# A fused attention and FFN block: moving the last q tile, two layer norms, PSUM banks and a scaling

## The chip, the cores and the metric

One Trainium2 chip, one core. The metric is the device time of one execution in microseconds, the median over the runs. Every matmul runs at the full granted TensorE clock (mean 1.000).

## The reference

One block with adaptive layer norm, linear attention and a SwiGLU FFN, on 2048 rows of 1024:

```python
mod = (silu(c) @ w_mod).reshape(1, 6, 1, -1); sa, ca, ga, sb, cb, gb = ...
h  = layernorm(x) * (1 + ca) + sa
q, k, v = split(h @ wqkv) into 32 heads of 32
phi(t) = where(t > 0, t + 1, exp(t)) + 1e-6
kv = sum_s phi(k) v ;  z = sum_s phi(k)                    # per head
o  = (phi(q) @ kv) / (phi(q) @ z + 1e-6)
x  = x + ga * (o @ wo)
h  = layernorm(x) * (1 + cb) + sb
x  = x + gb * ((silu(h @ w_gate) * (h @ w_up)) @ w_down)   # F = 3584
```

All inputs and the output are bfloat16.

## The kernel before

The program is a list of operations for five in-order queues (TensorE "pe", ScalarE "act", VectorE "dve", GpSimd "pool", and "sp", which issues the DMAs). A helper records every operation and derives the waits from the bytes, and for PSUM from the whole bank, that it touches. So nearly all instructions have the line of that helper, L176, and are told apart by their tiles. The order within a queue is the order in which the code calls the helpers.

**Stages.** The rows are cut into 4 chunks of 512 (each of 4 row tiles `st` of 128).

1. *Start and chunk 0's q (0 to 29 us).* Layer norm of chunk 0, transposes, and `q_phase_chunk0`: seven of the eight q tiles (`nt` 0 to 6) are accumulated in seven PSUM banks `qb = [1, 2, 3, 4, 6, 7, 5]`, one input slice `dt` at a time (`q_part`), while the modulation vectors are still being computed: `mod_sc` are 16 or 32 matmuls with one column into bank 0, `fin_sa` reads them out, `bias_mm` (32 one-column matmuls) and `bias_fin` give a bias for the q tiles. The eighth tile (`nt` 7) follows in bank 0. `h0_shift` then adds the shift to four slices of the transposed input `HT`. `q_phi` evicts a q tile with two ScalarE instructions (Exp into `E1`/`E1X`, Relu into `RL`/`RLX`), `q_min` and `q_add` make phi of them on VectorE (about 0.2 and 0.33 us an instruction) and write `PQT`.
2. *k of chunk 0, then chunks 1 to 3 (29 to 126 us).* Each group is 8 matmuls of 128x512. A chunk is 8 k groups and 8 q groups (chunk 0 has its q groups before). I write c1k2 for the k group 2 of chunk 1. `phi_evac` evicts a group: ScalarE's Exp into one of four slots of `E1` (for q a Relu too); after every second group `phi_flush` does VectorE's part of both: `min`, `min`, then for k one `scalar_tensor_tensor` each into `PKT` (it reads PSUM too, so a k group's bank comes free only there), for q one `tensor_tensor` each. `next_bank` gives the PSUM bank: a ring of eight for the first 40 groups, then a ring of five for chunk 3, because banks 0, 6 and 7 are kept for the next stage.
3. *Side work of stage 2.* The dictionaries `kside` (chunk 0's k), `s1`, `s2`, `s3` (chunks 1 to 3) say behind which group which helpers are called: the layer norm of the chunk after (`ln1_stats_ops`: two `bn_stats` and an aggregate on VectorE; `act_stats`: two passes of 1024 columns on ScalarE, Identity and Square with a sum; `ln1_xn`: the normalisation), its transposes by DMA (`th_dma`, one for each row tile, into `HT`), the scaling and shift of the eight slices of the transposed chunk (`th_mod(ch, dt)`; chunk 1's all on VectorE, of the others the odd ones on ScalarE), and a part of the modulation that VectorE sums up from a 2 MB block of `w_mod` in `STG` (`macc`, eight passes of 1024 columns into `ACC`). `macc_split` writes `MHL` and sends it through a DMA transpose; behind that in the DMA queue stands the load of the next 2 MB into `STG`, which chunk 3's `macc` needs.
4. *G (126 to 186 us).* 16 groups of 16 matmuls, `g_evac`, the reciprocal of the denominator, which goes out to memory and comes back broadcast as `RB` (two loads of four DMAs, 512 KB each), `scale_pq` (PQT times RB, one hg a time), `kvt_mm`, `m_mm`.
5. *Output projection, second layer norm and FFN (186 to 824 us).* 

The rings and the side work that matter here:

```python
return (1, 2, 3, 4, 6, 7, 5, 0)[i % 8] if i < 40 else i % 5 + 1        # next_bank
add(s2, 13, macc_split)
add(s2, 13, lambda: P.dma("stg1", STG[:], wmv[:, :, 4096:5120]))
add(s3, 4 + kt, lambda kt=kt: macc(STG, kt))                            # kt 0 to 7
```

Of the kernel before, what the change touches and what calls it, by code (L numbers as in the profile page):

```python
# [5 lines left out]
FP32 = mybir.dt.float32  # L6
BF16 = mybir.dt.bfloat16
U8 = mybir.dt.uint8
ACT = mybir.ActivationFunctionType
# [253 lines left out]
def bass_adaLN_cond__linear_attn_block__swiglu_ffn__prompt_kernel(  # L263
# [22 lines left out]
    with ExitStack() as es:  # L286
# [59 lines left out]
        RL = T("rl", 188 * KB, [128, 4, 512], BF16)  # L346
        E1X = T("e1x", 192 * KB, [128, 4, 512], BF16)
        RLX = T("rlx", 196 * KB, [128, 4, 512], BF16)
        ACC = T("acc", 192 * KB, [128, D], FP32)
        MHL = T("mhl", 196 * KB, [128, 2, D], BF16)  # L350
        MHLT = T("mhlt", 192 * KB, [128, 2 * NDT, 128], BF16)
# [351 lines left out]
        def next_bank():  # L703
            i = qk_ctr[0]
            qk_ctr[0] += 1
            return (1, 2, 3, 4, 6, 7, 5, 0)[i % 8] if i < 40 else i % 5 + 1

        def q_group(ch, nt):
            buf, bank = ch % 2, next_bank()
# [39 lines left out]
        def mod_row_b(bank, i, dst):  # L749
# [3 lines left out]
            P.wait_for("sp", [wr])  # L753
            P.dma("mdr%d" % i, dst[:], MDR[i].unsqueeze(0).to_broadcast([128, D]))

        def q_slot(nt):
            return (E1, RL) if nt < 4 else (E1X, RLX)

        def q_phi(nt, bank):
            for buf, fn_ in zip(q_slot(nt), (ACT.Exp, ACT.Relu)):  # L760
                P.act("activation", out=buf[:, nt % 4, :], in_=PS[:, bank, :], func=fn_, bias=BIASQ[:, nt:nt + 1])

        def q_min(nts):
            for nt in nts:
                e = q_slot(nt)[0][:, nt % 4, :]
                P.dve("tensor_scalar", out=e, in0=e, scalar1=1.0, scalar2=1e-6, op0=ALU.min, op1=ALU.add)

        def q_add(nts):
            for nt in nts:
                e, r = q_slot(nt)  # L770
                P.dve("tensor_tensor", out=PQT[:, nt, 0:512], in0=r[:, nt % 4, :], in1=e[:, nt % 4, :], op=ALU.add)

        def q_phase_chunk0():
            qb = [1, 2, 3, 4, 6, 7, 5]
            fin_ca(2, 2)
            for dt in (2, 3):
                h0_first(dt, "dve")
            for nts, dts in ((range(3), (0,)), (range(3), (1,)), ((3, 4, 5, 6), (0, 1))):
                for nt in nts:
                    q_part(nt, qb[nt], dts)  # L780
            for nt in range(7):
                if nt == 4:
                    mod_sc(WCA, 8, range(4, 8))
                    fin_ca(4, 4)
                    for dt in (4, 5):
                        h0_scale_only(dt)
                q_part(nt, qb[nt], (2, 3))
            act_stats(4, (0,))
            for nt in range(7):
                if nt == 6:  # L790
                    mod_sc(WSA, 0, range(6, 8))
                    fin_sa(6, 2)
                    for dt in (6, 7):
                        h0_scale(dt)
                q_part(nt, qb[nt], (4, 5))
            mod_sc(WSA, 0, range(4, 6))
            fin_sa(4, 2, True)
            for dt in (4, 5):
                h0_shift(dt)
            for nt in range(7):  # L800
                if nt == 2:
                    bias_mm((4, 5))
                q_part(nt, qb[nt], (6,))
            for nt in range(7):
                if nt == 1:
                    mod_sc(WSA, 0, range(4), range(4))
                if nt == 3:
                    mod_sc(WSA, 0, range(4), range(4, 8))
                    fin_sa(0, 4, True)
                    ln_ops[1][0]()  # L810
                if nt == 5:
                    bias_mm(range(4))
                    bias_fin()
                q_part(nt, qb[nt], (7,))
            ln_ops[1][1]()
            ln_ops[1][2]()
            ln1_rstd1(5)
            for i, dt in enumerate((4, 5, 0, 1, 2, 3, 6, 7)):
                P.pe("matmul", out=PS[:, 0, :], lhsT=WQK[:, dt, 896:1024], rhs=HT[:, 0, dt, :], start=(i == 0),
                     stop=(i == 7))  # L820
            for dt in range(4):
                h0_shift(dt)
            ln1_xn(5)
            th_dma(5)
            for nt in range(2):
                q_phi(nt, qb[nt])
            act_stats(4, (1,))
            for nt in range(2, 8):
                q_phi(nt, qb[nt] if nt < 7 else 0)
            for f in ln_ops[2]:  # L830
                f()
            act_var(4)
            pool_pow(4)
            for f in ln_ops[3]:
                f()
            ln1_rstd2(6)
            ln1_xn_sum(4)
            th_dma(4)
            q_min((0, 1))
            for st in (6, 7):  # L840
                ln1_xn(st)
                th_dma(st)
            q_add((0, 1))
            for nts in ((2, 3), (4, 5)):
                q_min(nts)
                q_add(nts)
            qk_ctr[0] = 0

        def add(d, k, f):
# [2 lines left out]
        kside = {}  # L852
        ln_ops = [ln1_stats_ops(4 + jj) for jj in range(4)]

        for c0 in (0, 256):
            for dt in range(NDT):
                add(kside, 1, lambda dt=dt, c0=c0: th_mod(1, dt, c0, c0 + 256))
        add(kside, 1, lambda: q_min((6, 7)))
        add(kside, 1, lambda: q_add((6, 7)))
        for jj, k in ((0, 3), (1, 4)):  # L860
            add(kside, k, lambda jj=jj: act_stats(10 + jj))
        q_phase_chunk0()
        for st in range(12, 16):
# [44 lines left out]
            add(s1, 2, lambda jj=jj: th_dma(8 + jj))  # L908
        for i, dt in zip([9, 9, 10, 10, 10, 11, 11, 11], range(NDT)):
            add(s1, i, lambda dt=dt: th_mod(2, dt))  # L910
        ln_half(3, s1, 8, 8, 11)
        for jj in range(4):
            add(s1, 13 + jj // 2, lambda jj=jj: ln1_xn(12 + jj))
            add(s2, 0, lambda jj=jj: th_dma(12 + jj))
        for dt in range(NDT):
            add(s2, 6 + dt, lambda dt=dt: th_mod(3, dt))
        for kt in range(NDT):
# [52 lines left out]
        def den():  # L970
            for hg in range(NHG):
                for ch in range(NCH):
                    P.pe("matmul", out=PS[32 * ch:32 * ch + 32, 7, :], lhsT=ZSEL[:, hg * 32:hg * 32 + 32],
                         rhs=PQT[:, hg, ch * 512:(ch + 1) * 512], start=(hg == 0), stop=(hg == NHG - 1),
                         skip_group_check=True)
            P.dve("tensor_scalar", out=DEN[:], in0=PS[:, 7, :], scalar1=1e-6, scalar2=None, op0=ALU.add)
            P.dve("reciprocal", out=RCP[:], in_=DEN[:])
            P.dve("tensor_copy", out=RCB[:], in_=RCP[:])
            wr = [P.dma("rdr%d" % ch, RDR[:, ch * 512:(ch + 1) * 512], RCB[32 * ch:32 * ch + 32, :])
                  for ch in range(NCH)]  # L980
            P.wait_for("sp", wr)
            for gh in range(2):
                outs = [RB[32 * hh:32 * hh + 32, 4 * gh:4 * gh + 4, :] for hh in range(4)]
                ins = [RDR.rearrange("(g x) s -> x g s", x=4)[hh, 4 * gh:4 * gh + 4].unsqueeze(0).to_broadcast([32, 4, S])
                       for hh in range(4)]

                def fn(e, outs=outs, ins=ins):
                    return [e.dma_start(out=o_, in_=i_) for o_, i_ in zip(outs, ins)]

                P.add("sp", fn, reads=[], writes=outs, lane="rb%d" % gh, ninc=4, tag="rb")  # L990

        def scale_pq(hg):
            P.dve("tensor_tensor", out=PQT[:, hg, :], in0=PQT[:, hg, :], in1=RB[:, hg, :], op=ALU.mult)
# [1 line left out]
        def kvt_mm(half):  # L995
            for h in range(4):
                for dt in range(NDT):
                    for g in range(4):
                        c0 = 512 * half + 128 * g + 32 * h
                        P.pe("matmul", out=PS[32 * g:32 * g + 32, 6, 32 * h:32 * h + 32], lhsT=WV[:, dt, c0:c0 + 32],  # L1000
                             rhs=G[:, dt, c0:c0 + 32], start=(h == 0 and dt == 0), stop=(dt == NDT - 1),
                             skip_group_check=True)
            P.dve("tensor_copy", out=KVT[:, half, :], in_=PS[:, 6, 0:128])

        def m_mm(half, nh, banks):
            for k in range(4):
# [31 lines left out]
        for g in range(16):  # L1038
            g_group(g)
            while ev < g + 1 - (3 if g < 4 else 2 if g < 6 else 1):  # L1040
                g_evac(ev)
                ev += 1
            if g == 0:
                z_row()
                for f in range(2):
                    wo_load(f)
            if g == 1:
                mod_red()
                mod_fin_col(2, True)
                den()  # L1050
            if 6 <= g <= 9:
                fold_ga(2 * (g - 6))
                fold_ga(2 * (g - 6) + 1)
            if g == 10:
                kvt_mm(0)
            if 11 <= g < 13:
                m_mm(0, g - 11, [MB, 7, G_BANKS[4], 6])
            if 7 <= g < 15:
                scale_pq(g - 7)
            if g == 10:  # L1060
                P.dma("stgx1", STGX[0][:], wmv[:, :, 3072:4096])
        g_evac(15)
# [185 lines left out]
```

## Time and profile before

| | |
|---|---|
| median of 3 runs | 827.69 us (827.62 to 828.37) |
| the profiled execution: its time, its span | 827.71 us, 826.0 us |
| TensorE busy, granted clock | 816.3 us, 1.000 |
| VectorE, ScalarE, GpSimd busy | 312.2, 197.0, 41.0 us |
| DMA | 119.32 MB |
| chain that ended last | 98% matmuls |

The span runs from the first to the last instruction; 1.7 us of the execution lie around it. Busy time is the union of an engine's instructions. Matmuls are pipelined: one of 128x512 shows as 0.38 us, but the next starts 0.216 us after it. A trace lacks a few per cent of the matmul records, so a missing start is not a pause.

### The profile page before, as it was taken

To read this page: it belongs to the slowest core of one execution; us is meant where nothing else is said; L and a number is where in the kernel's file an instruction comes from. 1 tells how busy PE (TensorE), PEld (TensorE's weight loads), DVE (VectorE), ACT (ScalarE), POOL (GpSimd) and SP (SyncE) were. 2 spreads that over 40 slices of the span, in tenths; PEclk is the share of its full clock that TensorE was granted. 3 is DMA by queue.
4 is the path that set the end of the run, shared out by engine and by line. 5 is a ranking of instruction groups with operands and counts; after the bars stand their busy time and mean duration, and the time that the engine had idled before them with its cause. 6 is when DMAs were issued, how large, how long until landed. Compare 5 with 4: busy or idle time off the path is not lost.

```text
span 826.0 us, 10436 instructions
## 1 busy us (share of the span) xinstructions
PE 816.3 (99%) x4243; PEld 375.9 (46%) x4322; DVE 312.2 (38%) x672; ACT 197.0 (24%) x338; POOL 41.0 (5%) x58
## 2 busy tenths in 40 slices
PE   8999999999999999999999999999999999999998
PEld 4544444444444444444444444444444444444444
DVE  5798988477945521111221112122111111221111
ACT  4758642123341111011111101111110111111011
POOL 1110000000130000020000003000000300000000
DMA  9969756865698995600455570045557004553000
GB/s 316 297 139 223 167 159 149 181 175 211 149 253 245 296 249 153 166 26 26 136 151 151 153 174 25 23 131 153 151 152 182 27 19 126 151 152 88 0 26 26
DMA packets 199392, 119.32 MB, mean 144 GB/s; under 512 B 58024, under 2 KB 183088, under 8 KB 199344
## 3 DMA queue, kind: packets, MB, share of 16 engines
q1 hardware_dynamic: 199328, 118.65, 53.8%
q8 instruction: 34, 0.56, 0.3%
q14 instruction: 14, 0.11, 0.0%
q10 hardware_dynamic: 16, 0.00, 0.0%
HBM read 100.67 MB, written 4.33 MB: 127 GB/s over the span
## 4 chain that ended last, share of the span: by engine, by line
PE 98%; issue 1%; DMA 0%; DVE 0%; POOL 0%; SPq 0%
PE ps L176 98%; DMA xres<-in_A_x_dram 0%; POOL rstd L176 0%; DVE xres L176 0%; DVE stats L176 0%; SPq L176 0%; DVE ht L176 0%; DVE ve L176 0%; DVE mv L176 0%; DVE modcol L176 0%
## 5 line engine op out<-in xcount | busy, mean ns | idle before, releaser
L176 PE MATMUL ps<-h2t,gug 128*128 128x512 bf16 x878 | 210.1, 379 | 0.9
L176 PE MATMUL ps<-h2t,guu 128*128 128x512 bf16 x878 | 209.9, 379 | 0.9
L176 DVE TENSOR_TENSOR at<-sg,ps 128x512 bf16<-128x512 bf16 x112 | 77.0, 687 | 282.8 <-PE ps L176 270.6
L176 ACT ACTIVATE sg<-ps 128x512 bf16<-128x512 f32 x112 | 66.9, 597 | 309.7 <-PE ps L176 298.3
L176 PEld LDWEIGHTS ps<-h2t,guu 128*128 128x128 bf16 x896 | 87.7, 98 | 105.7
L176 PEld LDWEIGHTS ps<-h2t,gug 128*128 128x128 bf16 x896 | 87.6, 98 | 105.5
L176 PE MATMUL ps<-wd_a,at 128*128 128x512 bf16 (+1 forms) x502 | 111.9, 377 | 0.5
L176 PE MATMUL ps<-ht,wqk 128*128 128x512 bf16 x499 | 110.7, 379 | 0.9 <-DVE ht L176 0.2
L176 PE MATMUL ps<-wd_b,at 128*128 128x512 bf16 (+1 forms) x377 | 84.6, 377 | 0.4
L176 PEld LDWEIGHTS ps<-wd_a,at 128*128 128x128 bf16 x512 | 50.1, 98 | 59.6
L176 DVE TENSOR_TENSOR ut<-att,gb_b 128x512 bf16<-128x512 bf16 (+1 forms) x32 | 13.6, 426 | 167.5 <-ACT att L176 167.5
L176 PEld LDWEIGHTS ps<-ht,wqk 128*128 128x128 bf16 x512 | 49.2, 98 | 58.9 <-DVE ht L176 1.0
L176 ACT ACTIVATE att<-ps 128x512 bf16<-128x512 f32 (+1 forms) x32 | 17.4, 591 | 182.1 <-PE ps L176 182.1
L176 PEld LDWEIGHTS ps<-wd_b,at 128*128 128x128 bf16 x384 | 37.6, 98 | 44.7
L176 PE MATMUL ps<-pk,xres 128*128 128x512 bf16 x250 | 55.4, 379 | 0.6 <-issue 0.5
L176 PE MATMUL ps<-mw,pqt 128*128 128x512 bf16 x249 | 55.4, 379 | 0.5 <-issue 0.2
L176 POOL TENSOR_SCALAR h2t<-h2t,modcol 128x512 bf16<-128x512 bf16 x32 | 26.5, 846 | 383.0 <-DMA h2t<-xn 383.0
L176 ACT ACTIVATE e<-ps 128x512 bf16<-128x512 f32 x56 | 33.3, 611 | 31.8 <-PE ps L176 15.8
L176 ACT ACTIVATE junk<-xres 128x1024 bf16<-128x1024 bf16 x26 | 27.6, 1063 | 45.9 <-DVE xres L176 34.2
L176 PEld LDWEIGHTS ps<-mw,pqt 128*128 128x128 bf16 x256 | 24.8, 98 | 30.0 <-issue 0.5
L176 PEld LDWEIGHTS ps<-pk,xres 128*128 128x128 bf16 x256 | 24.6, 98 | 30.1 <-issue 1.3
L176 DVE SCALAR_TENSOR_TENSOR xres<-ps,xres 128x512 bf16<-128x512 f32 x32 | 21.5, 688 | 11.6 <-PE ps L176 11.3
(111 smaller groups left out, 337.8 us busy)
## 6 DMA issues: line engine op xcount, KB each, us to landing
gug<-in_B_w_gate_dram SPq DMA_DIRECT2D x56, 512.0 KB, 4.0
guu<-in_B_w_up_dram SPq DMA_DIRECT2D x56, 512.0 KB, 5.3
xres<-in_A_x_dram SPq DMA_DIRECT2D x20, 256.0 KB, 4.4
rb<-recip_den SPq DMA_DIRECT2D x8, 512.0 KB, 11.7
stgx<-in_w_mod_dram SPq DMA_DIRECT2D x2, 2048.0 KB, 9.3
wd_a<-in_B_w_down_dram SPq DMA_DIRECT2D x4, 1024.0 KB, 7.7
out_dram<-xres SPq DMA_DIRECT2D x31, 128.0 KB, 1.7
xres<-in_A_x_dram SPq DMA_DIRECT2D x3, 1024.0 KB, 6.5
```

What stands on the lines that cost most here:

```text
L176: return getattr(e, method)(**kw)
```

## The change

Five things are moved; the arithmetic stays.

- *Chunk 0's q.* Tile 0 of q is finished first, ScalarE copies it as fp32 to a new tile `QRAW`, and the eighth tile is accumulated in the bank that this frees. Its eight matmuls stand between the pieces of the last shift products (`mod_sc`, `bias_mm`), where the last round of `q_part` stood. Both passes of `act_stats(4)`, its variance, `pool_pow(4)` and the normalisation of row tile 4 come earlier, before the q evictions. The evictions run in the order `QORD`.
- *Banks.* `next_bank` has other rings for the first 40 groups.
- *Chunk 1's scaling.* Still called behind c0k1, but with 8 half-width instructions for the slices 0 to 3 and 4 full-width ones for 4 to 7, in place of 16 halves; the last two pairs of chunk 0's q go behind c0k3 (before, only the last pair came this late, right behind the scaling); `act_stats(10)` and `(11)` one group later.
- *Chunk 3's layer norm.* From behind groups 8, 9 and 11 of chunk 1 to behind 12, 13 and 14; the normalisation from 13 and 14 to 15 and the first group of chunk 2; the transposes from behind c2k0 to behind c2k1.
- *RB.* Loads of 3, 3 and 2 hg; the third is issued by SP behind a wait for the eviction of `kvt_mm(0)`; `scale_pq(6)` and `(7)` at G groups 14 and 15 in place of 13 and 14.

```diff
         def next_bank():
...
-            return (1, 2, 3, 4, 6, 7, 5, 0)[i % 8] if i < 40 else i % 5 + 1
+            if i < 24:
+                return (0, 2, 3, 4, 6, 7, 5, 1)[i % 8]
+            if i < 40:
+                return (0, 2, 3, 4, 6, 1, 7, 5, 0, 2, 3, 1, 4, 6, 7, 5)[i - 24]
+            return i % 5 + 1
...
-            act_stats(4, (0,))
...
             for nt in range(7):
-                if nt == 1:
+                q_part(nt, qb[nt], (7,))
+                if nt == 0:
+                    P.act("activation", out=QRAW[:], in_=PS[:, qb[0], :], func=ACT.Copy)
+                    act_stats(4)
+            for i, dt in enumerate(range(NDT)):
+                if i == 1:
                     mod_sc(WSA, 0, range(4), range(4))
-                if nt == 3:
+                if i == 3:
                     mod_sc(WSA, 0, range(4), range(4, 8))
+                    ln_ops[1][0]()
                     fin_sa(0, 4, True)
-                    ln_ops[1][0]()
-                if nt == 5:
+                    ln_ops[1][1]()
+                    act_var(4)
+                    pool_pow(4)
+                if i == 5:
                     bias_mm(range(4))
                     bias_fin()
-                q_part(nt, qb[nt], (7,))
-            ln_ops[1][1]()
+                P.pe("matmul", out=PS[:, qb[0], :], lhsT=WQK[:, dt, 896:1024], rhs=HT[:, 0, dt, :], start=(i == 0),
+                     stop=(i == 7))
...
+            ln1_xn_sum(4)
+            th_dma(4)
             ln1_xn(5)
             th_dma(5)
...
-            q_add((0, 1))
-            for nts in ((2, 3), (4, 5)):
-                q_min(nts)
-                q_add(nts)
+            q_add(QORD[0:2])
+            q_pair(2)
...
-        for c0 in (0, 256):
-            for dt in range(NDT):
-                add(kside, 1, lambda dt=dt, c0=c0: th_mod(1, dt, c0, c0 + 256))
-        add(kside, 1, lambda: q_min((6, 7)))
-        add(kside, 1, lambda: q_add((6, 7)))
-        for jj, k in ((0, 3), (1, 4)):
+        for dt, c0, c1 in ([(dt, 0, 256) for dt in range(4)] + [(dt, 256, 512) for dt in range(4)]
+                           + [(dt, 0, 512) for dt in range(4, 8)]):
+            add(kside, 1, lambda dt=dt, c0=c0, c1=c1: th_mod(1, dt, c0, c1))
+        for i in (4, 6):
+            add(kside, 3, lambda i=i: q_pair(i))
+        for jj, k in ((0, 4), (1, 5)):
             add(kside, k, lambda jj=jj: act_stats(10 + jj))
...
-        ln_half(3, s1, 8, 8, 11)
+        ln_half(3, s1, 12, 12, 14)
         for jj in range(4):
-            add(s1, 13 + jj // 2, lambda jj=jj: ln1_xn(12 + jj))
-            add(s2, 0, lambda jj=jj: th_dma(12 + jj))
+            add(s1 if jj < 2 else s2, 15 if jj < 2 else 0, lambda jj=jj: ln1_xn(12 + jj))
+            add(s2, 1, lambda jj=jj: th_dma(12 + jj))
...
+            rb_load(0, 3)
+            rb_load(3, 6)
...
             if g == 10:
-                kvt_mm(0)
+                P.wait_for("sp", [kvt_mm(0)])
+                rb_load(6, 8)
...
-            if 7 <= g < 15:
+            if 7 <= g < 13:
                 scale_pq(g - 7)
+            elif g == 14:
+                scale_pq(6)
+            elif g == 15:
+                scale_pq(7)
```

Here `q_pair(i)` is `q_min` and `q_add` of the tiles `QORD[i:i + 2]`, and `ln_half(ch, d, k_act, k_dve, k_fin)` puts `act_stats`, `bn_stats` and the final sums of a chunk behind the groups `k_act`, `k_dve` and `k_fin`.

More of the change, by code (lines that the diff above doesn't have):

```diff
@@ L348, in bass_adaLN_cond__linear_attn_block__swiglu_ffn__prompt_kernel @@
         RLX = T("rlx", 196 * KB, [128, 4, 512], BF16)
+        QRAW = T("qraw", 202 * KB, [128, 512], FP32)
         ACC = T("acc", 192 * KB, [128, D], FP32)
@@ L754, in mod_row_b, with q_phi @@
             P.dma("mdr%d" % i, dst[:], MDR[i].unsqueeze(0).to_broadcast([128, D]))
+        QORD = (1, 2, 3, 4, 5, 6, 7, 0)
         def q_slot(nt):
-            return (E1, RL) if nt < 4 else (E1X, RLX)
-        def q_phi(nt, bank):
+            i = QORD.index(nt)
+            bufs = (E1, RL) if i < 4 else (E1X, RLX)
+            return [t[:, i % 4, :] for t in bufs]
+        def q_phi(nt, src):
             for buf, fn_ in zip(q_slot(nt), (ACT.Exp, ACT.Relu)):
-                P.act("activation", out=buf[:, nt % 4, :], in_=PS[:, bank, :], func=fn_, bias=BIASQ[:, nt:nt + 1])
+                P.act("activation", out=buf, in_=src, func=fn_, bias=BIASQ[:, nt:nt + 1])
         def q_min(nts):
             for nt in nts:
-                e = q_slot(nt)[0][:, nt % 4, :]
+                e = q_slot(nt)[0]
                 P.dve("tensor_scalar", out=e, in0=e, scalar1=1.0, scalar2=1e-6, op0=ALU.min, op1=ALU.add)
@@ L770, in q_add, with q_pair @@
                 e, r = q_slot(nt)
-                P.dve("tensor_tensor", out=PQT[:, nt, 0:512], in0=r[:, nt % 4, :], in1=e[:, nt % 4, :], op=ALU.add)
+                P.dve("tensor_tensor", out=PQT[:, nt, 0:512], in0=r, in1=e, op=ALU.add)
+        def q_pair(i):
+            q_min(QORD[i:i + 2])
+            q_add(QORD[i:i + 2])
         def q_phase_chunk0():
@@ L804, in q_phase_chunk0 @@
             for nt in range(7):
-                if nt == 1:
+                q_part(nt, qb[nt], (7,))
[4 more added lines that the diff above has]
+                if i == 1:
                     mod_sc(WSA, 0, range(4), range(4))
-                if nt == 3:
+                if i == 3:
                     mod_sc(WSA, 0, range(4), range(4, 8))
+                    ln_ops[1][0]()
                     fin_sa(0, 4, True)
-                    ln_ops[1][0]()
-                if nt == 5:
+                    ln_ops[1][1]()
+                    act_var(4)
+                    pool_pow(4)
+                if i == 5:
                     bias_mm(range(4))
                     bias_fin()
-                q_part(nt, qb[nt], (7,))
-            ln_ops[1][1]()
+                P.pe("matmul", out=PS[:, qb[0], :], lhsT=WQK[:, dt, 896:1024], rhs=HT[:, 0, dt, :], start=(i == 0),
+                     stop=(i == 7))
             ln_ops[1][2]()
             ln1_rstd1(5)
-            for i, dt in enumerate((4, 5, 0, 1, 2, 3, 6, 7)):
-                P.pe("matmul", out=PS[:, 0, :], lhsT=WQK[:, dt, 896:1024], rhs=HT[:, 0, dt, :], start=(i == 0),
-                     stop=(i == 7))
             for dt in range(4):
                 h0_shift(dt)
+            ln1_xn_sum(4)
+            th_dma(4)
             ln1_xn(5)
             th_dma(5)
[L825 to L829, printed above, removed]
+            for nt in QORD:
+                q_phi(nt, QRAW[:] if nt == 0 else PS[:, qb[nt % 7], :])
             for f in ln_ops[2]:
                 f()
-            act_var(4)
-            pool_pow(4)
             for f in ln_ops[3]:
@@ L836, in q_phase_chunk0 @@
             ln1_rstd2(6)
-            ln1_xn_sum(4)
-            th_dma(4)
-            q_min((0, 1))
+            q_min(QORD[0:2])
             for st in (6, 7):
@@ L981, in den, with rb_load, fn @@
             P.wait_for("sp", wr)
[L982 to L990, printed above, removed]
+            rb_load(0, 3)
+            rb_load(3, 6)
+        def rb_load(h0, h1):
+            outs = [RB[32 * x:32 * x + 32, h0:h1, :] for x in range(4)]
+            ins = [RDR.rearrange("(g x) s -> x g s", x=4)[x, h0:h1].unsqueeze(0).to_broadcast([32, h1 - h0, S])
+                   for x in range(4)]
+            def fn(e, outs=outs, ins=ins):
+                return [e.dma_start(out=o_, in_=i_) for o_, i_ in zip(outs, ins)]
+            P.add("sp", fn, reads=[], writes=outs, lane="rb%d" % h0, ninc=4, tag="rb")
         def scale_pq(hg):
@@ L1002, in kvt_mm @@
                              skip_group_check=True)
-            P.dve("tensor_copy", out=KVT[:, half, :], in_=PS[:, 6, 0:128])
+            return P.dve("tensor_copy", out=KVT[:, half, :], in_=PS[:, 6, 0:128])
         def m_mm(half, nh, banks):
```

## The prediction

> **What bounds the kernel now.** First the page: TensorE is busy for 99% of the span.
>
> ```profile
> span 826.0 us, 10436 instructions
> PE 816.3 (99%) x4243; PEld 375.9 (46%) x4322; DVE 312.2 (38%) x672; ACT 197.0 (24%) x338; POOL 41.0 (5%) x58
> ```
>
> No matmul is added or taken away, so only TensorE's waits can change the time. The waits of the weight loads from 12 us on say how much there is to win:
>
> ```profile
> PEld ps L176 <- DVE ht L176: 1.0, 6, 0.2
> PEld ps L176 <- DVE pkt L176: 0.5, 1, 0.5
> ```
>
> A weight load runs ahead of its matmul, so I read these waits from the starts of the matmuls, 215.8 ns apart in an unbroken row. Four starts are late by 36, 10, 133 and 11 ns: 0.19 us, at 44.67 us (c1k0 waits for the last scaled slice of HT) and 46.76 us (c1k2 waits for c0k2's eviction to free its bank). All other breaks behind 23 us are 57 ns (bias), 47 ns (a G group) and seven of 93 ns where the tile shape changes. The change can win 0.2 us, not more; the question is what it can lose. So next, how full the other engines are by stretch (columns: stretch, length, then busy us and instructions of PE, PEld, DVE, ACT, POOL):
>
> ```profile
> 62.00:83.60 21.60, 21.49 (x100) 9.80 (x100) 18.07 (x59) 17.61 (x33) 1.86 (x3) 1.00 1.06 228
> 83.60:101.20 17.60, 17.50 (x82) 7.94 (x82) 17.53 (x38) 12.79 (x23) 0.00 (x0) 1.00 0.65 154
> 101.20:110.80 9.60, 9.55 (x45) 4.37 (x45) 5.86 (x14) 2.98 (x5) 0.00 (x0) 1.00 1.03 292
> 110.80:127.30 16.50, 16.45 (x78) 7.50 (x77) 16.29 (x37) 9.58 (x18) 0.00 (x0) 1.00 0.28 54
> ```
>
> VectorE has no gap from 83.6 to 101.2 and again from 110.8 on. Between them it waits; its order of time says for what:
>
> ```profile
> 98.85 1.23 DVE L176 TENSOR_TENSOR mhl<-acc,mhl 128x1024 bf16<-128x1024 f32 x1
> ...
> 110.83 0.75 DVE L176 TENSOR_SCALAR acc<-stg,siluf 128x1024 f32<-128x1024 bf16 x1 [2.22 <-DMA stg<-in_w_mod_dram]
> 111.50 0.49 DVE L176 TENSOR_SCALAR e<-e 128x512 bf16<-128x512 bf16 x2
> 111.90 0.68 DVE L176 SCALAR_TENSOR_TENSOR pkt<-ps,e 128x512 bf16<-128x512 f32 x1
> ...
> 116.05 0.68 DVE L176 SCALAR_TENSOR_TENSOR pkt<-ps,e 128x512 bf16<-128x512 f32 x1
> ```
>
> and SP's:
>
> ```profile
> 100.10 1.94 SPq L176 DMA_TRANSPOSE mhlt<-mhl x1
> 102.09 0.99 SPq L176 DMA_DIRECT2D stg<-in_w_mod_dram x1
> ```
>
> This is one chain: the second load of STG is issued when MHL is done (100.08), lands 8.7 us later, and chunk 3's first `macc` waits for it in front of the evictions of c3k4 and c3k5 (111.90), with c3k6 behind (116.05). These free banks of the ring of five. Counting back from G's first matmul (126.25) by 215.8 ns each and 56 ns for `mod_row_b`: c3q1 starts at 114.11 in c3k4's bank, free at 112.58, cover 1.53; c3q3 starts at 117.56 in c3k6's bank, free at 116.73, cover 0.83. These two covers are the smallest that the change touches.
>
> **The change, part by part.**
>
> *Chunk 0's q.* The matmuls and their three one-column blocks stay the same in number. The copy to QRAW can start when tile 0 is done (24.83) and takes 0.6 to 0.72 us (a PSUM eviction, an fp32 result); the matmul that reuses its bank is due at 25.91, so it is hidden by 0.36; were it not, TensorE would wait the difference. The bias now comes 7 matmuls later: 7 x 0.216 = 1.51. ScalarE's q evictions start at 27.59 + 1.51 = 29.10; sixteen of them at 0.572 end at 38.25 (two now read fp32 from SBUF; between an Exp of 0.48 and an fp32 eviction of 0.67 that is -0.2 to +0.2 us, I take nothing). One row-sum pass of 1.03 that stood among them moves into idle time ahead. So c0k0's Exp starts at 38.25, before 37.77: 0.48 later. The first k group moves to bank 0, free when BIASQ is read at 29.01, due at 29.31: no wait. VectorE's shifts end at 30.38, needed from 30.18 to 30.83 in order, each 0.4 ahead. Normalisations 6 and 7 end at 35.96 and 36.42, so SP issues the last transposes at about 36.0 and 37.4 (36.33 and 37.69 now); they land by 41.8 as now.
>
> *Chunk 1's scaling.* VectorE begins it at 40.43 + 0.48 = 40.91. Sixteen halves took 4.11, 0.257 each; a full one of this kind has 0.33 (two at 67.51, 0.73 to the end of the second). So 8 x 0.257 + 4 x 0.33 = 3.38: done at 44.29 and the last slice at 44.37, needed at 44.63. The right halves begin at 41.94, just behind the last landing. c0k2's bank comes free at 45.4, before 46.69, due at 46.58. Both waits go: -0.19. But two q pairs of 1.08 now stand where one stood, so VectorE reaches chunk 1's first `bn_stats` at 50.48 + 0.48 - 0.73 + 1.08 = 51.31: **0.83 late**. The k evictions behind it have covers of 1.2 (c1k3) and more; c1q2, with 1.39 now, keeps about 0.4.
>
> A full scaling costs 0.073 more than a half in these rows, so most of the price is per instruction, 0.18. [...]
>
> *Chunk 3's layer norm.* Its two `act_stats` (1.17 + 1.06 each) stood in ScalarE's queue ahead of chunk 2's scaling:
>
> ```profile
> 65.02 0.81 ACT L176 ACTIVATE ht<-ht,modcol 128x512 bf16<-128x512 bf16 x1
> 65.73 1.05 ACT L176 ACTIVATE junk<-xres 128x1024 bf16<-128x1024 bf16 x1
> ...
> 75.80 1.17 ACT L176 ACTIVATE e<-ps 128x512 bf16<-128x512 f32 x2
> ```
>
> One ran from 61.83 while the transposes landed (63.96). Now these land at 63.96 + 0.83 = 64.79 and ScalarE, free at about 63.7, has nothing else: it waits 1.1. From 64.83 it has four scalings (0.71), six q evictions (0.955) and both `act_stats` (2.23): 2.84 + 5.73 + 4.46 = 13.03, so c1q7's Relu ends near 78.0 (now 75.99). VectorE, in order, finishes that pair and normalises tiles 12 to 15 from 78.40, now:
>
> ```profile
> 74.47 1.91 DVE L176 TENSOR_SCALAR xres<-xres,mv,rstd 128x1024 bf16<-128x1024 bf16 x4
> ```
>
> Behind them come c2k0 to c2k3 (3.26), the first `macc` (0.67) and c2k4, c2k5 (1.63): 78.40 + 1.84 + 3.26 + 0.67 + 1.63 = 85.80, where 83.62 stands now. **VectorE is 2.18 late as it enters the stretch without a gap.** ScalarE's own 2 us cost nothing: with eight banks the smallest cover there is 3.6 (c2k5, in the new ring six groups behind the last use of its bank; 5.5 now).
>
> *Where that lateness goes.* Chunk 3's transposes are issued from 78.9, the last lands near 86.2, its first scaling is due on VectorE at 87.0: hidden. The scaling of slice 6 ends at 97.14 + 2.18 = 99.32; c3k0 needs it at 99.67: hidden by 0.3. MHL: 100.08 + 2.18 = 102.26. STG lands at 110.81 + 2.18 = 112.99. c3k4's bank: 112.58 + 2.18 = 114.76, and a matmul starts 0.07 behind that (46.69 to 46.76): 114.83, due at 114.11 - 0.19 = 113.92. **Wait 0.91.** c3k6's: 116.73 + 2.18 + 0.07 = 118.98, due at 117.56 - 0.19 + 0.91 = 118.28. **Wait 0.70.** c3q4 has 1.95 now: no wait.
>
> *RB.* The reciprocal chain starts from VectorE and moves with it (2.2); the loads of three hg move less before the first scaling, so RB's first part lands near 161.0 (161.25 now). Behind SP's new wait stand the third load, `stgx1` and the reload of x, which itself waits for G's last groups; `stgx1` lands near 183, used at 195.8. The last RB load starts at about 170.6 and is used near 182: for 1 MB, a quarter of what took 21.7 from 149.30, I take 5.5. Scalings 6 and 7 (1.22 each) end before G's last group. Nothing on the path.
>
> *Sum.* +0.91 + 0.70 - 0.19 = +1.42, that is 2.18 - 0.76. On the profiled execution's 827.71 (span 826.0 and 1.7 around it), equal to the median within 0.02: **829.1 us**, 0.17% over. About 0.2%, 1.66 us, is what a measurement of this kernel can tell from no change.
>
> **The rivals.**
>
> *The lateness is absorbed (827.5, chance 0.14).* VectorE is idle for 3.5 of the 21.6 us from 62 to 83.6. If it catches up to 0.64 late or less, neither cover is used up and only the -0.19 stays. Against it: that idle time is waiting for ScalarE's evictions, and ScalarE is what runs late.
>
> *The scaling block ends as late as ever (slower: 829.9, chance 0.30).* Place: VectorE from 40.91 on. The 0.33 is from a stretch with other traffic; bounds for a full one are 0.27 (512 columns with one scalar, at 22.94) and two halves, 0.51. At 0.51 the block takes 4.11 again, all behind it is 0.73 later, and the end too, since every term of the chain moves with it: 2.18 + 0.73 - 0.76 = +2.15. At 0.27 it is +1.18. From 0.24 over my value, 0.39 an instruction, the change is slower by more than 0.2%. A late landing of chunk 1's last transpose (41.84 now, and the order of the four changes) pushes the block's second half, and with it the end, by the same rule; for it speaks that the landing has only 0.1 to spare. [...]
>
> *Faster by more than 0.2% (chance 0.02).* All breaks that could vanish are under 0.4 us.
>
> **How the numbers follow.** The forecast, 829.1, has 0.54; its own spread of some 0.4 (the terms are read to 0.1 to 0.2 each, five in a row) leaves 0.08 of that above 829.35. So slower by over 0.2%: 0.38; within: 0.14 + 0.46 = 0.60; faster 0.02. The forecast's own range is 828.7 to 829.5; 827.5 to 830.2 takes in the absorbed case and most of the slow one.
>
> **What would show it.** Right: no late matmul starts near 44.7 and 46.8; tile 12's normalisation at 78.4; MHL done near 102.3 and STG landing near 113; two waits of a weight load on `pkt`, at about 114 and 118, of 0.9 and 0.7; all later stages 1.4 later. Wrong: a wait for HT at 43 to 45 or at 99.7, a first scaling behind 41, a wait in G for `g`, `kvt` or RB, or MHL done before 100.7.

## The result, and the profile after

| | before | changed |
|---|---|---|
| median of 18 runs each, us | 828.02 (827.59 to 828.51) | 829.46 (828.90 to 830.24) |
| ratio, 95% interval | | 1.0018 (1.0011 to 1.0024) |
| the profiled execution: its time, its span | 827.71, 826.0 | 830.09, 828.3 |

The changed kernel is 1.44 us slower; the forecast was 829.1, with 827.5 to 830.2 as range. The profiled execution lies 0.63 above the median of its kernel. In it the first matmul of `mod_sc(WSA, ...)` starts at 21.71 in place of 21.20, before any moved step can act on TensorE. The traces further down have offsets from -0.1 to +1.0 there, with the old front as well as with the new one. So where I compare two traces, I subtract this offset, 0.51 for the changed kernel; the lines of views, and times marked as raw, are as the trace has them.

The page, and the waits of the weight loads from 12 us on (total us, times, longest us):

```profile
span 828.3 us, 10516 instructions
PE 821.6 (99%) x4322; PEld 376.1 (45%) x4322; DVE 311.9 (38%) x668; ACT 197.2 (24%) x339; POOL 40.8 (5%) x58
...
PEld ps L176 <- DVE pkt L176: 3.1, 4, 1.5
...
PEld ps L176 <- DVE ht L176: 0.7, 2, 0.5
```

TensorE's busy time is 5.3 above before's because this trace has all the records of matmuls (4322 against 4243): the trace of e10 has all of them too, and 821.8 busy in a span of 827.5. The waits for `pkt` went from one of 0.5 to four, 3.1 in all. A weight load begins to wait ahead of its matmul's turn (at c3q1 the load waits 1.50, and the matmul starts 1.17 late), so the cost is read from the late starts of the matmuls again (raw times of the late starts):

| late start | before | after |
|---|---|---|
| c1k0 for HT, c1k2 for c0k2's bank | 0.04 + 0.13 (and 0.02) | none |
| c3k0 for slice 6 of HT, at 100.37 | none | 0.19 |
| c3k7 for c3k2's bank, at 111.23 | none | 0.06 |
| c3q1 for c3k4's bank, at 115.87 | none | 1.17 |
| c3q3 for c3k6's bank, at 120.01 | none | 0.68 |
| G, at 172.66 | 0.05 | none |

Each of the four new ones brings 0.01 more at the next matmul: 2.14 new, 0.24 gone, +1.90. With the offset of 0.51 that is 2.41; the two spans lie 2.39 apart (828.35 less 825.96).

VectorE's order of time shows the chain that the forecast named:

```profile
79.42 1.91 DVE L176 TENSOR_SCALAR xres<-xres,mv,rstd 128x1024 bf16<-128x1024 bf16 x4
...
102.03 1.23 DVE L176 TENSOR_TENSOR mhl<-acc,mhl 128x1024 bf16<-128x1024 f32 x1
...
114.05 0.75 DVE L176 TENSOR_SCALAR acc<-stg,siluf 128x1024 f32<-128x1024 bf16 x1 [2.26 <-DMA stg<-in_w_mod_dram]
114.72 0.49 DVE L176 TENSOR_SCALAR e<-e 128x512 bf16<-128x512 bf16 x2
115.12 0.68 DVE L176 SCALAR_TENSOR_TENSOR pkt<-ps,e 128x512 bf16<-128x512 f32 x1
...
119.26 0.68 DVE L176 SCALAR_TENSOR_TENSOR pkt<-ps,e 128x512 bf16<-128x512 f32 x1
```

Tile 12's normalisation starts 4.95 later than in before (74.47, raw), the `mhl` subtraction 3.18 later (98.85), and the first macc still waits for STG, 3.22 later (110.83). Less the offset these are 4.44, 2.67 and 2.71. Behind it stand, as before, the two evictions that c3q1 and c3q3 need. The reason is visible on ScalarE:

```profile
65.81 0.81 ACT L176 ACTIVATE ht<-ht,modcol 128x512 bf16<-128x512 bf16 x1 [1.42 <-DMA ht<-xres]
...
71.52 1.08 ACT L176 ACTIVATE junk<-xres 128x1024 bf16<-128x1024 bf16 x1
```

It idles 1.42 for chunk 2's transposes, in time that a row-sum pass used to fill, and does the passes from 71.52 on, ahead of evictions that VectorE waits for. By stretch (columns: stretch, length, then busy us and instructions of PE, PEld, DVE, ACT, POOL, clock, DMA share, GB/s):

```profile
83.60:101.20 17.60, 17.57 (x82) 7.78 (x81) 17.60 (x40) 12.37 (x23) 0.00 (x0) 1.00 0.97 198
...
110.80:127.30 16.50, 14.97 (x70) 6.41 (x69) 14.06 (x32) 7.71 (x14) 0.00 (x0) 1.00 0.49 122
```

VectorE is full in the first stretch, so it can't catch up there; in the second TensorE is busy for 1.5 less than before (16.45).

### The profile page after: what moved, and what is told of

Same layout as the page of the kernel before. It is cut to its first block, busy times and chain, and to the rows that moved or that the text cites. A ratio compares the mean times of both kernels' runs of the same rounds, so it can differ in the third digit from the quotient of the medians.

```text
span 828.3 us, 10516 instructions
## 1 busy us (share of the span) xinstructions
PE 821.6 (99%) x4322; PEld 376.1 (45%) x4322; DVE 311.9 (38%) x668; ACT 197.2 (24%) x339; POOL 40.8 (5%) x58
## 4 chain that ended last, share of the span: by engine, by line
PE 93%; DVE 4%; DMA 2%; ACT 0%; issue 0%; SPq 0%; POOL 0%; ACTq 0%
PE ps L176 93%; DVE acc L176 1%; DMA stg<-in_w_mod_dram 1%; DVE pkt L176 1%; DMA xres<-in_A_x_dram 1%; DVE e L176 1%; DVE xres L176 0%; DVE pqt L176 0%; ACT ht L176 0%; DVE mhl L176 0%; SPq L176 0%; ACT e L176 0%; POOL rstd L176 0%; DVE ht L176 0%; ACT rl L176 0%
## 5 line engine op out<-in xcount | busy, mean ns | idle before, releaser
L176 PE MATMUL ps<-ht,wqk 128*128 128x512 bf16 x512 | 112.4, 379 | 1.6 <-DVE pkt L176 1.5
```

Source lines behind the costliest of these rows:

```text
L176: return getattr(e, method)(**kw)
```

## The experiments

Each ratio is against the kernel before in the same set of runs, whose medians were 828.12 to 828.39.

| run | what it has of the change | median, us | ratio, 95% interval | late starts from 30 us on |
|---|---|---|---|---|
| e1_macc_late | all, macc two groups later | 827.69 | 0.9996 (0.9987 to 1.0005) | none |
| e2_ln_only | layer norm | 829.93 | 1.0021 (1.0012 to 1.0030) | c1: 0.18; c3q1 0.39; c3q3 0.68; G 0.95 |
| e3_front_only | q order, rings, scaling | 829.01 | 1.0010 (1.0001 to 1.0019) | c2k0 0.47 and 0.26; G 0.76 |
| e4_rb_only | RB | 828.18 | 1.0000 (0.9991 to 1.0009) | c1: 0.18 |
| e5_split_late | RB; STG load delayed | 829.26 | 1.0014 (1.0005 to 1.0022) | c1: 0.17; c3q1 1.04; c3q3 0.68 |
| e6_late_macc_rb_undone | all but RB, macc later | 829.11 | 1.0009 (1.0000 to 1.0018) | c3k0 0.04; c3k7 0.05; G 1.37 |
| e7_rb_undone | all but RB | 830.72 | 1.0027 (1.0018 to 1.0037) | c3q1 0.91; c3q3 0.68; G 0.90 |
| e8_ln_and_rb | layer norm and RB | 828.64 | 1.0004 (0.9995 to 1.0013) | c1: 0.21; c3q1 0.33; c3q3 0.68 |
| e9_halves | all, 16 half scalings | 830.35 | 1.0025 (1.0015 to 1.0034) | c1k0 0.78; c3k0 0.06; c3k7 0.06; c3q1 0.96; c3q3 0.68 |
| e10_rb_no_wait | all, macc later, no pause in RB | 829.16 | 1.0007 (0.9998 to 1.0016) | c3k0 0.06; c3k7 0.06; G 0.72 |
| e11_scale_later | as e6, scalings one group later | 829.13 | 1.0009 (1.0001 to 1.0018) | G 1.60 |

The 0.09 breaks at changes of tile shape, the 0.01 behind each wait and the bias break ahead of 30 us are left out.

### Are the two bank waits the loss? (e1, e5)

```diff
 e1, on the changed kernel
-            add(s3, 4 + kt, lambda kt=kt: macc(STG, kt))
+            add(s3, 6 + kt, lambda kt=kt: macc(STG, kt))
 e5, on the kernel before with the RB part
-        add(s2, 13, macc_split)
-        add(s2, 13, lambda: P.dma("stg1", ...))
+        add(s2, 15, macc_split)
+        add(s2, 15, lambda: P.dma("stg1", ...))
```

> The changed kernel with one thing more: chunk 3's eight macc passes stand two groups later, behind c3k6 to c3q5 in place of c3k4 to c3q3. All other steps are as in the change. Theory (cover): VectorE runs late, so the second load of STG lands late, and the first macc stands in front of the evictions of c3k4 to c3k7; with the macc behind them VectorE does these evictions while it waits for STG. The two bank waits of the changed kernel (1.17 at c3q1, 0.68 at c3q3) go; what stays is 0.2 at c3k0 for slice 6 and 0.05 at c3k7. Against the kernel before that is +0.25 - 0.19 - 0.05: 827.8 to 828.1, and 1.4 to 1.9 less than the changed kernel. Rival (the loss is elsewhere: in the front, in the rings or in G): the time stays at 829.3 to 829.6. Rival (VectorE is the bound of the end of chunk 3): the eight passes, two groups later, end later, and the time rises to 830 or more.

Measured: 827.69, below the expected 827.8 to 828.1, and no late start at all in stage 2. VectorE is nearly as late as in the changed kernel (less the offset of 0.26 the `mhl` subtraction starts 2.3 later than in before, there 2.67), but now evicts c3k4 while STG is on its way, and waits 0.56 in place of 2.26:

```profile
111.52 0.68 DVE L176 SCALAR_TENSOR_TENSOR pkt<-ps,e 128x512 bf16<-128x512 f32 x1
...
113.38 0.75 DVE L176 TENSOR_SCALAR acc<-stg,siluf 128x1024 f32<-128x1024 bf16 x1 [0.56 <-DMA stg<-in_w_mod_dram]
```

So the lateness costs next to nothing by itself; it costs through the macc that stands in front of evictions. Both rivals fall. That the small waits at c3k0 and c3k7 are gone too is not the macc's doing, for they stand ahead of it: e6 and e10, with the same late macc, have them at 0.04 to 0.06. In e1's trace the transposes landed earlier (the table of the section on why the prediction was right). This version is faster than the changed kernel; against the kernel before its 0.4 us are within the interval. By the traces it can be 0.24 faster, the waits that the change removes.

> The kernel before with the change's RB part, and in place of its other parts only this: macc_split of chunk 2 and the STG load behind it stand behind c2q7 in place of c2q5. MHL is then done near 102.2 in place of 100.1, and STG lands near 112.9. Theory (cover): the late landing of STG alone makes the two waits, 0.65 at c3q1 and 0.69 at c3q3, with no layer norm moved: 829.3 to 829.5, +1.3. Rival (the waits come from VectorE's evictions being late in chunk 2, or from the rings): no late start behind 100, 828.1.

Measured: 829.26, 1.05 over its kernel before where 1.3 was expected, and the same two waits, 1.04 and 0.68, with neither the layer norm nor the rings touched. MHL's subtraction starts at 102.01 (raw; 101.03 less the offset, and done at 102.26), and STG is there at

```profile
114.29 0.75 DVE L176 TENSOR_SCALAR acc<-stg,siluf 128x1024 f32<-128x1024 bf16 x1 [2.52 <-DMA stg<-in_w_mod_dram]
```

less an offset of 0.98: 113.31, 0.4 behind the 112.9 expected, which is the 0.39 by which the first wait exceeds 0.65. A late STG alone makes the waits: the RB part, which e5 has too, makes none (e4). The second wait is 0.68 in every run that has one: once c3q1 has waited for the eviction of c3k4, the one of c3k6 follows on VectorE at a fixed distance (4.14 us in the changed kernel).

### The parts one by one (e2, e3, e4)

e2 has only the lines of chunk 3's layer norm (`ln_half(3, s1, 12, 12, 14)` and the four lines for the normalisation and the transposes behind it); e3 is the changed kernel with those lines and the RB part as before; e4 has the RB part alone.

> The kernel before with only chunk 3's layer norm moved, as in the change. Theory (cover): VectorE does not start chunk 1 late here, so the lateness at the second macc is about 1.4 to 1.9 in place of 2.6 in the changed kernel; no wait or one of up to 0.35 at c3q1, one of 0.6 to 0.7 at c3q3; the 0.19 at 44.7 and 46.8 stays: +0.6 to +1.05 over the kernel before, 828.6 to 829.1. Rival (the layer norm alone makes all of it): +1.4 or more. Rival (the front makes all of it, through VectorE's two q pairs): no change, 828.0.

> The kernel before with only the new order of chunk 0's q, the new rings and chunk 1's new scaling; chunk 3's layer norm and RB are as before. Theory (cover): the waits at 44.7 and 46.8 go (-0.19) and none comes at c3q1 or c3q3; but ScalarE still has a row-sum pass of chunk 3 ahead of chunk 2's scaling, which now ends later than c2k0 needs slices 5 and 7: waits of 0.5 and 0.3 near 72 and 73. Together +0.6: 828.6. Rival (the layer norm's move makes the whole loss and the front is a gain): -0.2, 827.8. Rival (the front itself loses, as its first matmuls start 0.5 later in the trace of the changed kernel): +0.5 with no late start near 72.

> The kernel before with only the loads of RB as in the change: 3, 3 and 2 hg, SP's wait for the eviction of kvt_mm(0), and the last two scalings one group later. Theory (cover): nothing of it lies on the path; the late start of 0.05 at 172.4 goes; 828.0 within 0.2. Rival (the third load, behind SP's wait, makes G or the output projection wait): slower, with late starts between 170 and 190.

e4 is as expected. e2 and e4 have the old front, and their first modulation matmuls start 0.68 and 0.37 later than in the trace of before: the late start comes without the change too. e2 and e3 have the chunk waits where they were expected (0.39 and 0.68; 0.47 and 0.26), but both are slower than expected (829.93 for 829.1 at most, 829.01 for 828.6). Their traces have one late start more, of 0.95 and 0.76 in G, that none of my theories had. In e3 ScalarE does a row-sum pass (`junk`) between chunk 2's scalings (`ht`):

```profile
66.77 0.81 ACT L176 ACTIVATE ht<-ht,modcol 128x512 bf16<-128x512 bf16 x1
67.48 1.05 ACT L176 ACTIVATE junk<-xres 128x1024 bf16<-128x1024 bf16 x1
...
72.32 1.52 ACT L176 ACTIVATE ht<-ht,modcol 128x512 bf16<-128x512 bf16 x2
```

so the last odd slices are done behind 73 and c2k0 waits. The layer norm's move clears this queue, and pays with the later STG. One part removes a wait that the other makes.

### A wait in G that nothing in the trace released (e6, e7, e8)

e6 is e1 with the RB part as before, e7 the changed kernel with the RB part as before, e8 the kernel before with the layer norm and the RB part.

> The changed kernel with chunk 3's macc two groups later, and the RB part as before: two loads of four hg. Theory (RB cover): in the kernel before the first scaling waits for RB until 161.28, 35.0 behind G's first matmul, and a late start of 0.05 at 172.4 shows that this cover is used up; the reciprocal chain runs 1.4 later here, and a load of four hg takes 12.0 from issue to first use where one of three takes 9.4. So a wait of 1.2 to 1.3 near 172.5: 828.8 to 829.1. Rival (the RB part is neutral, as in the run that had it alone): 827.7, no late start there.

> The changed kernel with the RB part as before. Theory (RB cover): besides the waits at c3q1 and c3q3 there is one of 0.7 to 1.0 near 174, as in the run with the layer norm alone: 830.2 to 830.5. Rival (the RB part is neutral): 829.4, as the changed kernel.

> The kernel before with the layer norm of chunk 3 moved and the RB part, without the new front, rings and scaling. Theory (two covers): the waits at c3q1 (0.1 to 0.4) and c3q3 (0.69) of the run with the layer norm alone stay, its 0.95 near 174 goes: 828.8 to 829.1. Rival (the 0.95 has another cause, such as the transposes): 829.9 with the wait near 174.

The late starts in G are near what was expected: 1.37 (for 1.2 to 1.3), 0.90 and none. The medians fit less well: e7's 830.72 lies 0.2 above its range, e8's 828.64 0.2 below, e6's 829.11 at the edge. With RB loaded as before, the change would have cost about 1 more: 0.90 by e7's trace, 1.07 by the medians (e7's 2.51 over its kernel before, less 1.44; each is uncertain by 0.5 to 0.8). But the mechanism in these expectations, VectorE held up by the first scaling, was a guess, and the waits of the weight loads speak against it. From 30 us on, e6 has

```profile
PEld ps L176 <- issue: 4.7, 10, 1.7
```

where e1 has

```profile
PEld ps L176 <- issue: 3.5, 10, 0.4
```

"Issue" means that no semaphore was seen to release it. In each of the seven traces with this wait the late matmul is the sixth of a G group; the waits for a bank, as at c3q1 and c3q3 in the changed kernel (1.17 and 0.68), stopped the first of a group.

### VectorE or the instruction queue? (e10, e11)

```diff
 e10, on e1
             rb_load(3, 6)
+            rb_load(6, 8)
...
-                P.wait_for("sp", [kvt_mm(0)])
-                rb_load(6, 8)
+                kvt_mm(0)
 e11, on e6 (stgx1 at g == 11 too, in place of 10)
-            if 7 <= g < 15:
-                scale_pq(g - 7)
+            if 8 <= g < 16:
+                scale_pq(g - 8)
```

> The changed kernel with chunk 3's macc two groups later and RB in loads of 3, 3 and 2 hg, but without SP's wait: the third load is issued right behind the second. So RB's first part is as early as in the change, and the traffic of all three loads runs on without a pause. Two readings of the wait in G (0.05 before, 0.8 to 1.4 in the runs with two loads of four) stand against each other. Fetch: the trace marks it as a wait for nothing it shows, at the sixth matmul of a group, and a 16 KB packet of the instruction queue ends 1.2 to 1.4 ahead of the restart in each of these runs; it stands behind RB's packets. Then the wait is back, 0.8 to 1.4 near 173: 828.5 to 829.1. Scaling: VectorE's evictions are late behind the first scalings by RB; then, with RB's first part early, there is no wait: 827.7.

> The run with the late macc and RB in two loads of four hg, with the eight scalings by RB each one G group later (groups 8 to 15 in place of 7 to 14), and the load of stgx1, which needs four of them done, one group later too. VectorE then does the evictions of G ahead of the scaling that waited for RB. Fetch: the wait of 1.2 to 1.4 near 173 stays, as the loads are the same: 828.9 to 829.2. Scaling: VectorE is no longer held up by RB in front of these evictions, and the wait goes or falls under 0.3: 827.7 to 828.0.

Both waits are there: 0.72 in e10, though RB's first part is used 33.8 behind G's first matmul (35.0 before), and 1.60 in e11, though VectorE had no eviction queued behind a scaling: it sat idle until 171.60, and TensorE's late matmul was due at 172.49. First e11's TensorE, then its VectorE:

```profile
171.41 1.25 PE L176 MATMUL ps<-pk,xres 128*128 128x512 bf16 x5
174.09 2.12 PE L176 MATMUL ps<-pk,xres 128*128 128x512 bf16 x9 [1.43 <-issue]
...
171.60 1.29 DVE L176 CAST mw<-ps 128x512 bf16<-128x512 f32 x2 [1.63 <-PE ps L176]
```

e10's wait is just under the 0.8 to 1.4 expected, its median, 829.16, just above 829.1; e11's time is as expected, its wait above the 1.2 to 1.4. The scaling falls; the reading that is left is the packet of the instruction queue. On the page of before, this queue has 34 packets and 0.56 MB, 16 KB each:

```profile
q8 instruction: 34, 0.56, 0.3%
```

The times of the packet near the wait (raw, from the trace's DMA packets), and G's length, from its first matmul to the output projection's:

| run | packet starts, after G's first matmul | packet ends, us | TensorE goes on, us | late start | G's length |
|---|---|---|---|---|---|
| e1 | 41.42 | 168.93 | | none | 59.55 |
| changed | 41.36 | 171.34 | | none | 59.54 |
| before | 43.73 | 171.26 | 172.66 | 0.05 | 59.62 |
| e10 | 44.54 | 172.93 | 174.17 | 0.72 | 60.28 |
| e3 | 44.48 | 173.43 | 174.81 | 0.76 | 60.32 |
| e7 | 44.82 | 173.65 | 174.86 | 0.90 | 60.46 |
| e2 | 44.86 | 174.10 | 175.29 | 0.95 | 60.50 |
| e6 | 45.18 | 173.25 | 174.55 | 1.37 | 60.95 |
| e11 | 45.37 | 172.72 | 174.09 | 1.60 | 61.16 |

Where DMA is free the packet starts at 41.4 (41.35 to 41.57 in e4, e5, e8 and e9 too, and none of them waits). Where RB's loads run on it starts 2.3 to 4.0 later, 0.9 to 1.3 before the last of them lands (in before 169.98 and 170.98, in e11 171.51 and 172.76), and TensorE goes on 1.2 to 1.4 behind the packet's end. In both kernels the packet starts near 170 (169.98 before, 170.07 changed). In 168 to 170 us, just ahead of it, the DMA share (last column but one) is, in the kernel before and then in the changed one:

```profile
168.00:170.00 2.00, 2.00 (x11) 0.90 (x10) 2.00 (x4) 0.00 (x0) 0.00 (x0) 1.00 0.91 182
```

```profile
168.00:170.00 2.00, 2.00 (x133) 1.35 (x130) 2.00 (x3) 0.00 (x0) 0.00 (x0) 1.00 0.02 4
```

So what the RB part brings is, above all, the pause in front of its third load: e10 has the smaller loads without the pause, and still 0.72 of the 1.37 that e6 has with two loads of four. That TensorE waits for this very packet is read from the order in time, the same in all traces; no run moved the packet alone.

### The price of a scaling instruction (e9)

```diff
-        for dt, c0, c1 in ([(dt, 0, 256) ...] + [(dt, 256, 512) ...] + [(dt, 0, 512) for dt in range(4, 8)]):
+        for dt, c0, c1 in [(dt, c, c + 256) for c in (0, 256) for dt in range(8)]:
```

> The changed kernel with chunk 1's scaling in sixteen halves, as before; all else as in the change. Theory (cover): the block is 0.7 longer, so slices reach c1k0 late (0.3 at the first, 0.04 at each of the others, 0.6 together, between 43 and 46), and VectorE and all behind it are 0.7 later: 0.1 to 0.2 more at c3k0 and c3q1 together. Sum +0.74 over the changed kernel: 830.2. [...] Rival (the block is off the path): 829.4 to 829.5.

Measured: 830.35, 0.52 more over its kernel before than the changed kernel has; 0.74 was expected, and the intervals (0.5 to 0.8 to either side) don't part that from a block that is off the path. The trace does. The changed kernel's block, then e9's:

```profile
41.47 3.54 DVE L176 TENSOR_SCALAR ht<-ht,modcol 128x256 bf16<-128x256 bf16 x12
```

```profile
41.44 4.19 DVE L176 TENSOR_SCALAR ht<-ht,modcol 128x256 bf16<-128x256 bf16 x16
```

It takes 4.19 in place of 3.54, 0.16 for each of the four instructions, and c1k0 waits 0.78. It is on the path. The growth that was expected further down isn't in this trace: c3q1 waits 0.96 and c3k0 0.06, less than the 1.17 and 0.19 of the changed kernel's.

## Why the prediction was right, step by step

The mechanism and the sign of each term held in stage 2; the reason given for G did not. Times less the offset (0.51, and -0.05 for e7, which is the same program up to G):

| step | predicted | changed | e7 |
|---|---|---|---|
| c0k0's Exp | 38.25 | 38.32 | 38.33 |
| scaling block starts | 40.91 | 40.96 | 40.97 |
| first `bn_stats` of chunk 1 | 51.31 | 51.44 | 51.40 |
| ScalarE's first scaling of chunk 2 | 64.83 | 65.30 | 65.00 |
| tile 12 normalised from | 78.40 | 78.91 | 78.61 |
| second macc | 85.80 | 86.28 | 85.97 |
| STG is there (start of the first macc) | 112.99 | 113.54 | 113.01 |
| wait at c3q1 | 0.91 | 1.17 | 0.91 |
| wait at c3q3 | 0.70 | 0.68 | 0.68 |

- *Chunk 0's q.* Right: 0.07 off. The copy to QRAW (0.60, done at 25.41) is hidden, as the matmul that reuses its bank starts at 25.91; the two evictions that read fp32 from SBUF take 0.62 each in place of 0.57.
- *Chunk 1's scaling.* Right: 3.45 to the next instruction against 3.38, and both old waits are gone. The rival in which the block ends as late as ever didn't happen; e9 is that rival, and slower. A scaling instruction costs 0.16 by e9, for the 0.18 read from the rows of before.
- *Chunk 3's layer norm.* Right in kind: ScalarE idles where I said, and VectorE enters the full stretch late. The term that was mis-sized is the landing of chunk 2's transposes: 65.30 in this trace, 65.00 in e7 and 64.98 in e1, for 64.83 predicted. I moved the old landing by VectorE's 0.83 and took its own duration as fixed. In the changed kernel the last of these transposes is issued at 61.62 (less the offset), 0.98 later than before in place of 0.83, and takes 3.58 to land in place of 3.32; its scaling follows 0.11 behind in place of the 0.04 that I took. Together that is the 0.47, which goes about one for one down the chain to STG; the wait at c3q1 grows by 0.26 alone, because c3k0 and c3k7 have held TensorE for 0.27 by then.
- *Where the lateness goes.* A cover is the time by which a step is ready before it is needed. Two were overrun there: slice 6 for c3k0 by 0.19 (I had left 0.3, and a lateness of 0.5 came), and c3k7 by 0.06, which I hadn't listed. So one of the signs that I had named for being wrong, a wait for HT at 99.7, is in this trace. In e7, with the earlier landing, neither wait is there and both predicted ones are met to 0.02. Six traces have this front and this layer norm: e1, e7 and e11 have the first scaling of chunk 2 at 64.92 to 65.00 and no wait at c3k0 or c3k7; the changed kernel, e6 and e10 have it at 65.16 to 65.30 and both waits. So the trace's +1.90 is a late case of the same chain. The median's +1.44 is near the predicted +1.42, but its interval is 0.9 to 2.0, and so close a hit is in part luck. (A reading to set right: STG's 8.7 us run from its issue at 102.09, not from the end of MHL at 100.08; the sum uses the shift alone and isn't touched.)
- *RB.* "Nothing on the path" was right for the changed kernel, and its reason was not. I filed the 47 ns at 172.66 under breaks of G and asked only whether a scaling would be late. It was the end of a cover: with the two loads as before, the lateness that I had predicted would have cost 0.90 there (e7). The change removes this wait with its own RB part, which I did not see; that the term came out as nothing was luck.
- *The absorbed case* has its trace in e1: no wait, and a time within 0.1% of the kernel before. It came with the macc behind the evictions, not with a VectorE that catches up.

## What to carry to other kernels

Where one engine is 99% busy, a moved step is priced by the covers it eats: follow the lateness to the next load that is issued behind it, and to what stands behind the wait for that load in an in-order queue. If lateness can't be avoided, try to move the waiting step behind the evictions; in e1 this one edit took the whole loss away. A break of a few hundredths of a microsecond in an otherwise unbroken row is worth a cause: it can be a cover that has just run out, as the 0.05 in G was, and then further delay is paid (up to 1.60 here).

## What the runs showed of the hardware that I had not expected

- In G TensorE stood for up to 1.60 us (e11) with no semaphore seen to release it. A 16 KB packet of the instruction queue that met RB's loads started 2.3 to 4.0 us later than on a free DMA, and in each of the seven traces with a late start there TensorE went on 1.2 to 1.4 us behind the packet's end. In the six traces in which the loads paused there is none. That TensorE waited for the packet is read from this order in time alone.
- The same program's transposes of a chunk landed 0.3 us apart in two traces (first scaling at 65.00 in e7 and 65.30 in the changed kernel, the same program up to G), and the start of the first modulation matmuls varied by 1.0 us between traces (21.15 to 22.18).
